# Fused linear attention and MLP: weight loads behind units 2, 3, 5 and 6, input loads in one fixed order

## Chip, cores and metric

One core of one Trainium2 chip. The metric is the device time of one execution in microseconds (us), as the median of the runs.

## What is computed

Two layers in a row on a batch of 8, with 8 heads, 576 positions and head width 64. The attention turns q and k into 256 positive features each and multiplies; the MLP normalises the joined heads (512 wide), goes up to 2048, cuts at zero, comes back to 512 and adds its input.

```python
def phi(x):
    proj = np.einsum('bhsd,df->bhsf', x, w_phi)
    proj = proj - np.max(np.abs(proj), axis=-1, keepdims=True)
    return np.concatenate([np.exp(proj), np.exp(-proj)], axis=-1)
q_p, k_p = (phi(q), phi(k))
kv = np.einsum('bhsf,bhsd->bhfd', k_p, v)
z = np.sum(k_p, axis=2)
num = np.einsum('bhsf,bhfd->bhsd', q_p, kv)
den = np.einsum('bhsf,bhf->bhs', q_p, z)[..., None] + 1e-06
x = num / den                      # then heads joined: (8, 576, 512)
xn = (x - mu) / np.sqrt(var + 1e-06) * g_ln
out = x + np.maximum(xn @ w_ch1, 0.0) @ w_ch2
```

## The kernel before

**Pairs, units, groups.** The batch is taken as four pairs of two. A pair's attention is 8 units (0 to 7 are pair 0, 8 to 15 pair 1, and so on); two units that share their loaded data are a group (g0 to g3 are pair 0, g4 to g7 pair 1). The 576 positions are 512 in the main loads and a rest of 64, the tails, which are loaded for many heads at once.

**One unit.** TensorE (PE) turns k and q with an identity (`qkT_ps`, L525; in pairs 1 to 3 a DMA transpose, L508, does it from a bf16 copy `qkb`). It projects them (`pm<-wbk` for k, `pm<-wbq` for q, L555, and `pt`, L648). VectorE (DVE) takes the maxima (L574), ScalarE (ACT) the exponentials (`EB`, `ea`), GpSimd (POOL) scales v into `vv` (L617 to L626), PE forms `kv` (L675) and then `num` (L704), DVE divides, and POOL writes the result into `x` (L728). The tails go the same way in small pieces: `xT_ps<-ident,kx` and `xT_ps<-ident,qx` (L394), then `px` (L404, L411).

**The MLP** of a pair takes 9 tiles of 128 rows in three rounds of three: centred tiles `xc`, turned to `xT`, the first layer `hT_ps` (L962, weights `w_98`), and the second layer `ch_ps` (L994, weights `w_99`). The MLP of one pair is interleaved with the attention of the next; the MLP of the last pair stands alone at the end.

**Buffers.** Inputs k and q lie in three buffers `qk_82`, `qk_83`, `qk_84`, v in `v_85`, `v_86`, `v_87`; group g uses buffer g modulo 3. The tails have two buffers each, by the pair's parity: `kx_90`, `qx_88`, `vx_92` for pairs 0 and 2, `kx_91`, `qx_89`, `vx_93` for pairs 1 and 3.

**Who loads.** Nearly all inputs are issued by SyncE (SP), whose queue is worked off in order: an issue that waits for a buffer holds all behind it, the DMA transposes and the stores too. The eight weight loads, 512 KB each as bf16, four of the first layer and four of the second, are issued by POOL (`load_w1`, `load_w2`, L284) from between its own work. A small memset of `kx_91` (L1139), put behind unit 4's `vv` on POOL, is the gate of pair 1's first loads.

**What sets the order.** `Order` (from L41) is a planner that runs while the kernel is built. Each step is added with an engine, an estimated time, a rank, and what it reads and writes; `run` then fixes the order of every engine by a list schedule over these estimates. A load is two steps: the issue on its queue, and the transfer on a resource "DMA" (SP and ACT loads) or "CAST" (POOL loads), whose times in the planner are independent of each other. While the flag `chained` is true, each SP load also writes a key "chain", so that loads are issued in the order in which the code adds them; after the loads of g5 it is set to False. The weights' places are a table from a unit to the loads that follow its `vv`:

```python
WEIGHTS = {0: (0,), 1: (1, 2), 2: (3,), 3: (4,), 4: (5,), 5: (6,), 6: (7,)}
```

Of the kernel before, what the change touches and what calls it, by code (L numbers as in the profile page):

```python
# [33 lines left out]
class Order:  # L34
# [73 lines left out]
    def run(self):  # L108
        waiting, free, room, events, done = {}, {}, self.room, [], []
        rows = False  # L110

        def offer(op):
            heapq.heappush(events, (op.ready, 1, op.number, op, None))

        for op in self.ops:
            for engine in op.alts:
                waiting.setdefault(engine, [])
                free.setdefault(engine, 0.0)
            if not op.left:
                offer(op)  # L120
        now = 0.0
        while events:
            now = events[0][0]
            while events and events[0][0] <= now + 1e-9:
                _, kind, _, op, _ = heapq.heappop(events)
                if kind == 1:
                    for engine in op.alts:
                        key = op.ready if engine in ("DMA", "CAST") else op.rank
                        heapq.heappush(waiting[engine], (key, op.number, op))
                elif kind == 0:  # L130
                    for name, n in op.release or ():
                        room[name] += n
            for engine, queue in waiting.items():
                if free[engine] > now + 1e-9 or not queue:
                    continue
                passed, held, op = [], set(), None
                while queue:
                    item = heapq.heappop(queue)
                    op = item[2]
                    if op.taken:  # L140
                        op = None
                        continue
                    if op.acquire is None or (
                        op.acquire[0] not in held and room[op.acquire[0]] >= op.acquire[1]
                    ):
                        break
                    held.add(op.acquire[0])
                    passed.append(item)
                    op = None
                for item in passed:  # L150
                    heapq.heappush(queue, item)
                if op is None:
                    continue
                op.taken, op.at = True, (now, engine)
                if op.acquire:
                    room[op.acquire[0]] -= op.acquire[1]
                end = now + op.alts[engine]
                if engine == "PE" and op.rows != rows:
                    rows = op.rows
                    end += 0.1  # L160
                lag = LAG[engine] if op.lag is None else op.lag
                free[engine] = end
                done.append((op, engine))
                heapq.heappush(events, (end, 2, op.number, op, None))
                heapq.heappush(events, (end + lag, 0, op.number, op, None))
                for o in op.users:
                    same = len(o.alts) == 1 and engine in o.alts
                    o.ready = max(o.ready, end + (0.1 if same else lag))
                    o.left -= 1
                    if not o.left:  # L170
                        offer(o)
        assert len(done) == len(self.ops)
        for op, engine in done:
            if op.emit:
                op.emit(engine)
        return now
# [3 lines left out]
def kernel(  # L180
# [71 lines left out]
    def early(kw):  # L252
        names = [name for name, _ in kw.get("release") or ()] + [kw.pop("frees", "")]
        return ahead[0] + (E_B if "B" in names else 0.0) + (E_A if "A" in names else 0.0)

    def add(engine, us, rank, emit, **kw):
        ahead_of = early(kw)
        sched.add(
            {engine: us}, rank, (lambda e: emit()) if emit else None, early=ahead_of, **kw
        )  # L260
# [16 lines left out]
    chained = [True]  # L277

    def dma(queue, rank, nbytes, dst, src, r=(), w=()):
        eng = ENG[queue]  # L280
        key = ("dma", len(sched.ops))

        def emit():
            eng.dma_start(out=dst() if callable(dst) else dst, in_=src() if callable(src) else src)  # L284

        chain = ["chain"] if queue == "SP" and chained[0] else []
        add(queue, {"SP": 0.55, "ACT": 0.55, "POOL": 0.84}[queue], rank, emit, r=r, w=(key, *w, *chain), lag=0.0)
        if queue == "POOL":
            add("CAST", 4.8, rank, None, r=(key,), w=w)
        else:  # L290
            rate = 240.0 if chained[0] else 330.0
            add("DMA", nbytes / rate / 1000.0, rank, None, r=(key,), w=w)

# [814 lines left out]
    load_tails(q, 0, [0, 1], "SP", 3.6)  # L1110
    moe_V = start(6)
    GATE = 4
    WEIGHTS = {0: (0,), 1: (1, 2), 2: (3,), 3: (4,), 4: (5,), 5: (6,), 6: (7,)}
    for n in range(NU + 2):
        V = start(n)
        step = start(n + 1) - V
        if n < NU:
            u = units[n]
            g, pair = u["g"], u["pair"]
            if n == 0:  # L1120
                a_trans(u, V)
            if u["uu"] == 0:
                if pair:
                    tails(g, V - 0.5 * step, None, True, g)
                    tails(g, V - 0.3 * step, [u["h"], u["h"] + 1], False, 64 + g)
                elif u["b"] == 0:
                    tails(g, V + 0.05, None, True, g)
                else:
                    tails(g, V, None, True, 8 + g)
            if pair == 0 and u["b"] == 1:  # L1130
                u["qjob"] = tails(g, V + 0.2 * step, [u["h"], u["h"] + 1], False, n)
            if pair:
                a_main(u, V, (1, 0))
            else:
                a_main(u, V, (1,))
            a_side(u, 1, V + 0.1 * step)
            if n == GATE:
                kx1 = kx_bufs[1]
                add("POOL", 0.1, V, lambda: nc.gpsimd.memset(kx1[:, :, 0:1], 0.0),  # L1139
                    r=[("vv", 0, n % 2)], w=[k_ for s_ in range(H) for k_ in tail_keys(1, s_, "k")])  # L1140
            for i_ in WEIGHTS.get(n, ()):
                after = [("vv", 0, n % 2)]
                if i_ < NW:
                    load_w1(i_, V, after)
                else:
                    load_w2(i_ - NW, V, after)
        if 0 < n <= NU:
            a_kv(units[n - 1], V + 0.2 * step)
        if n + 1 < NU:
            a_trans(units[n + 1], V + 0.3 * step)  # L1150
        if n < NU:
            if pair == 0:
                a_main(u, V + 0.35 * step, (0,))
            a_side(u, 0, V + 0.35 * step)
        if 0 < n <= NU:
            nums(units[n - 1], 0, V + 0.4 * step)
        if n < NU:
            a_feat(u, V + 0.5 * step)
        if 0 < n <= NU:
            w_ = units[n - 1]  # L1160
            nums(w_, 1, V + 0.6 * step)
            nums(w_, 2, V + 0.7 * step)
            if w_["pair"] == 0 and w_["b"] == 1:
                nums(w_, 3, V + 0.8 * step)
            pr, i = pairs[w_["pair"]], w_["i"]
            ahead[0] = E_X
            if w_["pair"] == 0 and i == 3:
                ahead[0] = E_X0
                for r in range(TILES0):
                    x_trans(pr, r, x_stats(pr, r, V), V)  # L1170
            if i == H - 1:
                pr["V"] = V + 0.9 * step
                ahead[0] = E_MOE
                moe_V = moe(pr, moe_V)
            ahead[0] = E_ATT
        gs = []
        if n % HG == 1 and n // HG + 3 != NGRP:
            gs.append(n // HG + 3)
        if n == GATE:
            gs = [NGRP] + gs  # L1180
        for g_ in gs:
            if g_ < NG:
                if g_ % NGRP == 0:
                    for i_, t_ in enumerate((k, q, v)):
                        load_tails(t_, g_ // NGRP, None, "SP", V + 0.1 * i_)
                for i_, t_ in enumerate((k, q, v)):
                    load_main(t_, g_, [0, 1], "SP", V + 0.5 + 0.1 * i_)
            if g_ == NGRP + 1:
                chained[0] = False
    ET = mybir.EngineType  # L1190
    with tc.manual_schedule(engines={ET.PE, ET.DVE, ET.Activation, ET.Pool, ET.SP}):
        sched.due()
# [31 lines left out]
```

## Time and profile before

| what | value |
|---|---|
| median of 3 runs | 400.43 us (400.22 to 401.17) |
| the profiled execution's own time | 402.7 us |
| its span, first to last instruction | 400.9 us |
| PE busy | 351.3 us (88%) |
| DVE, ACT, POOL busy | 278.4, 246.1, 210.8 us |
| moved by DMA | 52.69 MB, of it read from HBM 37.03 MB |
| mean granted TensorE clock | 0.982 |

The profiled execution is 2.3 us above the median. The shares are means over a run of unlike stages: start with only attention, a long middle in which attention and MLP alternate, and an end with only MLP. So the stretches are to be read one by one. A PE instruction shown as waiting for "issue" waits for something that the profile doesn't name.

### The profile page before, as it was taken

Reading aid. Unit: us, or ns where it says so; the run is one execution under the profiler, and the core shown is the slowest. Engines: PE = TensorE matmul, PEld = TensorE weight load, DVE = VectorE, ACT = ScalarE, POOL = GpSimd, SP = SyncE. Lnnn points to the kernel's source line nnn. Section 1 sums busy time; section 2 is a strip of 40 time slices with the busy share of each in tenths; the row PEclk is TensorE's granted clock in tenths of the full one; section 3 lists DMA queues with packets and bytes.
Section 4 is the critical chain, followed back from the end, with each engine's and each line's share of the span. In section 5 each row is a group of like instructions: output and inputs, shape, how many; then the busy total and the mean of one; then the engine's idle time right before and its main releaser. Section 6 shows DMA issues by size and latency. Waiting matters only on the chain. (4 is left out here: it accounts for less than half of the span.)

```text
span 400.9 us, 8845 instructions
## 1 busy us (share of the span) xinstructions
PE 351.3 (88%) x3283; PEld 208.7 (52%) x3332; DVE 278.4 (69%) x658; ACT 246.1 (61%) x511; POOL 210.8 (53%) x371
## 2 busy tenths in 40 slices
PE   3853586879999798999999999899999999999994
PEld 1632354536566454655655655465656545555541
DVE  3792989997779769887688898967768787010111
ACT  3993867769686743686777854966667505533310
POOL 4896796776544654975356675844445663000000
PEclk9996979999999999999999999999999999999999
DMA  7999799969547694692727524822200034110102
GB/s 196 318 228 250 164 220 316 274 158 225 158 91 117 171 226 124 151 191 54 213 54 210 132 41 105 173 42 54 52 28 28 29 92 93 39 54 26 51 31 78
DMA packets 88604, 52.69 MB, mean 131 GB/s; under 512 B 55024, under 2 KB 83824, under 8 KB 88560
## 3 DMA queue, kind: packets, MB, share of 16 engines
q1 hardware_dynamic: 83488, 47.07, 47.9%
q0 software_dynamic: 4224, 4.19, 6.3%
q10 hardware_dynamic: 848, 0.85, 0.7%
q8 instruction: 26, 0.43, 0.5%
q14 instruction: 18, 0.15, 0.1%
HBM read 37.03 MB, written 9.44 MB: 116 GB/s over the span
## 5 line engine op out<-in xcount | busy, mean ns | idle before, releaser
L962 PE MATMUL hT_ps<-xT,w 128*128 128x384 bf16 x768 | 150.2, 327 | 6.3 <-ACT KV L682 1.9
L994 PE MATMUL ch_ps<-w,hT 128*128 128x512 bf16 x536 | 141.2, 379 | 4.4 <-DVE numc L716 1.4
L972 ACT ACTIVATE hT<-hT_ps 128x384 bf16<-128x384 f32 x126 | 61.7, 492 | 74.4 <-PE hT_ps L962 73.8
L962 PEld LDWEIGHTS <-w 128*128 128x128 bf16 x768 | 71.4, 98 | 59.0 <-issue 8.7
L728 POOL TENSOR_TENSOR x<-numc,rden 128x192 bf16<-128x192 f32 (+1 forms) x112 | 51.0, 465 | 74.0 <-DVE rden L722 68.2
L574 DVE TENSOR_REDUCE m<-pm 128x8 f32<-128x1024 f32 x64 | 76.5, 1210 | 6.1 <-PE pm L555 5.9
L994 PEld LDWEIGHTS <-hT 128*128 128x128 bf16 x576 | 52.8, 98 | 50.7 <-DVE numc L716 2.5
L654 ACT ACTIVATE ea<-pt 128x1024 bf16<-128x1024 f32 x64 | 63.2, 1039 | 8.2 <-PE pt L648 6.8
L603 ACT ACTIVATE EB<-pm 128x1024 bf16<-128x1024 f32 x64 | 64.1, 1028 | 2.4 <-DVE m L574 2.4
L1001 DVE SCALAR_TENSOR_TENSOR o<-ch_ps,rstd,x 128x512 f32<-128x512 f32 x36 | 26.6, 742 | 52.7 <-PE ch_ps L994 39.7
L617 POOL TENSOR_TENSOR vv<-v,emk 128x512 bf16<-128x512 f32 x32 | 33.5, 1048 | 30.1 <-ACT emk L590 21.9
L710 DVE TENSOR_TENSOR numc<-num,emq 128x195 f32<-128x195 f32 (+1 forms) x96 | 32.9, 347 | 22.0 <-PE num L704 17.3
L970 DVE TENSOR_SCALAR hT<-hT_ps 128x384 bf16<-128x384 f32 x66 | 35.5, 542 | 8.2 <-PE hT_ps L962 7.2
L704 PEld LDWEIGHTS <-ea 128*128 128x128 bf16 x512 | 28.6, 99 | 18.7 <-issue 3.0
L704 PE MATMUL num<-KV,ea 128*128 128x65 bf16 x512 | 32.4, 196 | 3.1 <-DVE numc L716 1.9
L716 DVE TENSOR_TENSOR numc<-numc,num 128x195 f32<-128x195 f32 (+1 forms) x100 | 33.9, 344 | 1.5
L617 POOL TENSOR_TENSOR vv<-v,en 128x512 bf16<-128x512 f32 x32 | 33.4, 1045 | 0.4 <-DVE en L610 0.3
L861 POOL TENSOR_TENSOR xd<-x,mv 128x512 f32<-128x512 bf16 x19 | 20.8, 1094 | 11.1 <-DVE mv L848 10.0
L847 DVE BATCH_NORM_STATS2 st<-x 128x6 f32<-128x512 bf16 x36 | 24.3, 674 | 3.1 <-POOL x L728 3.1
L865 POOL TENSOR_TENSOR xc<-xd,gln 128x512 bf16<-128x512 f32 x19 | 25.3, 1331 | 1.5
L648 PE MATMUL pt<-qkT,wbk 128*128 128x512 bf16 x55 | 18.0, 397 | 8.0 <-DVE m L574 6.5
L675 PE MATMUL kv<-vv,EB 128*128 128x65 bf16 x512 | 24.8, 199 | 0.0
(67 smaller groups left out, 382.3 us busy)
## 6 DMA issues: line engine op xcount, KB each, us to landing
out_dram<-o SPq DMA_DIRECT2D x32, 256.0 KB, 2.4
qk<-in_k_dram SPq DMA_DIRECT2D x28, 256.0 KB, 4.1
v<-in_v_dram SPq DMA_DIRECT2D x28, 256.0 KB, 4.1
qk<-in_q_dram SPq DMA_DIRECT2D x26, 256.0 KB, 5.4
w<-in_moe_w_ch_dram POOLq DMA_DIRECT2D x8, 512.0 KB, 10.1
qk<-in_k_dram SPq DMA_DIRECT2D x2, 512.0 KB, 12.3
qk<-in_q_dram SPq DMA_DIRECT2D x2, 512.0 KB, 12.6
v<-in_v_dram SPq DMA_DIRECT2D x2, 512.0 KB, 15.0
```

The lines of the kernel that those rows point to most:

```text
L574: nc.vector.reduce_max(out=u["m", i].rearrange("p (c e) -> p e c", e=2), in_=u["pm", i], axis=AX.X, apply_absolute_value=True,)
L603: nc.scalar.activation(u["EB"][:, t].rearrange("p c f -> p (c f)"), u["pm", 1].rearrange("p e c f -> p (e c f)"), AF.Exp, scale=(1.0, -1.0 ...
L617: nc.gpsimd.tensor_tensor(out=u["vv"][:, t, 0:MX, 0:D], in0=vb[:, uu, :].rearrange("p (c d) -> p c d", d=D), in1=bcast(e[:, 0:MX], 2, D), ...
L654: nc.scalar.activation(u["EA"][:, t, :], u["pt"], AF.Exp, scale=(1.0, -1.0)[t])
L704: nc.tensor.matmul(ps[:, t, i, :], lhsT, rhs, start=(j == 0), stop=(j == len(terms) - 1))
L710: nc.vector.tensor_tensor(out=st["numc"][:, 0:nch], in0=st["ps"][:, 1], in1=bcast(em_of(), 2, D1), op=ALU.mult,)
L716: nc.vector.tensor_add(out=st["numc"][:, 0:nch], in0=st["numc"][:, 0:nch], in1=st["ps"][:, 0])
L728: nc.gpsimd.tensor_tensor(out=dst, in0=st["numc"][:, i : i + cnt, 0:D], in1=bcast(st["rden"][:, i : i + cnt], 2, D), op=ALU.mult,)
L962: nc.tensor.matmul(st["ps"][:, 0:cols], w1_sb[:, kc, jj * P : (jj + 1) * P], pr["xT", r][:, kc, 0:cols], start=(kc == 0), stop=(kc == KC - 1),
L970: nc.vector.tensor_relu(h_sb[:, 0:cols], st["ps"][:, 0:cols])
L972: nc.scalar.activation(h_sb[:, 0:cols], st["ps"][:, 0:cols], AF.Relu)
L994: nc.tensor.matmul(ch[t], hT[r, jj][:, rt * P : (rt + 1) * P], w2_sb[:, jj, :], start=(jj == 0), stop=(jj == JC - 1),)
```

## The change

It moves the weight loads in the table, two each behind units 2, 3, 5 and 6. It leaves `chained` true to the end, so all input loads are issued in the order of the code. And it changes the planner's estimates: one rate of 340 for SP and ACT loads where it was 240 or 330, 4.2 for a weight load where it was 4.8, and a transfer that starts while a weight load runs is taken to go at a quarter of its rate for that time. Since the planner's times change, all engines' orders change with them. The computation and every load's size stay.

```diff
@@ Order.run
                 op.taken, op.at = True, (now, engine)
                 if op.acquire:
                     room[op.acquire[0]] -= op.acquire[1]
-                end = now + op.alts[engine]
+                us = op.alts[engine]
+                if engine == "DMA" and free.get("CAST", 0.0) > now:
+                    shared = free["CAST"] - now
+                    us = 4.0 * us if 4.0 * us <= shared else us + shared * 0.75
+                end = now + us
@@ dma
         if queue == "POOL":
-            add("CAST", 4.8, rank, None, r=(key,), w=w)
+            add("CAST", 4.2, rank, None, r=(key,), w=w)
         else:
-            rate = 240.0 if chained[0] else 330.0
-            add("DMA", nbytes / rate / 1000.0, rank, None, r=(key,), w=w)
+            add("DMA", nbytes / 340.0 / 1000.0, rank, None, r=(key,), w=w)
@@
     GATE = 4
-    WEIGHTS = {0: (0,), 1: (1, 2), 2: (3,), 3: (4,), 4: (5,), 5: (6,), 6: (7,)}
+    WEIGHTS = {2: (0, 1), 3: (2, 3), 5: (4, 5), 6: (6, 7)}
@@
             if g_ == NGRP + 1:
-                chained[0] = False
+                pass
```

Lines of the changed kernel are 3 or 4 higher than those before. Three places show what it moves.

POOL, from unit 0's second `vv` (before) and from the end of unit 1 (changed) to the first weight loads that stand there. First before:

```order
L617 TENSOR_TENSOR vv<-v_85,en 128x8x64
L622 CAST vv<-en 128x8
L626 TENSOR_TENSOR vv<-vx_92,en 128x130
L284 DMA w_98<-in_moe_w_ch_dram 128x4x512
L617 TENSOR_TENSOR vv<-v_85,emk 128x8x64
L622 CAST vv<-emk 128x8
L626 TENSOR_TENSOR vv<-vx_92,emk 128x130
```

The change, where unit 2 (`v_86`) is the first with weights behind it:

```order
L731 TENSOR_TENSOR x_100<-numc,rden 128x64 x2
L620 TENSOR_TENSOR vv<-v_86,emk 128x8x64
L625 CAST vv<-emk 128x8
L629 TENSOR_TENSOR vv<-vx_92,emk 128x130
L620 TENSOR_TENSOR vv<-v_86,en 128x8x64
L625 CAST vv<-en 128x8
L629 TENSOR_TENSOR vv<-vx_92,en 128x130
L731 TENSOR_TENSOR x_100<-numc,rden 128x3x64
L288 DMA w_98<-in_moe_w_ch_dram 128x4x512 x2
```

The four loads of the first layer stood behind units 0, 1, 1 and 2 and stand behind 2, 2, 3 and 3; those of the second stood behind 3, 4, 5 and 6 and stand behind 5, 5, 6 and 6.

SP, from the last load of pair 0 (`v_85` of g3) on. Before:

```order
L284 DMA v_85<-in_v_dram 128x4x256
L284 DMA kx_90<-in_k_dram 64x8x64 x2
L284 DMA kx_91<-in_k_dram 64x8x64
L284 DMA qk_82<-in_k_dram 128x2x256
L284 DMA kx_91<-in_k_dram 64x8x64
L284 DMA qk_82<-in_k_dram 128x2x256
L284 DMA qx_89<-in_q_dram 64x8x64
L284 DMA qk_82<-in_q_dram 128x2x256
```

The change:

```order
L288 DMA v_85<-in_v_dram 128x4x256
L288 DMA kx_91<-in_k_dram 64x8x64 x2
L288 DMA qx_89<-in_q_dram 64x8x64 x2
L288 DMA vx_93<-in_v_dram 64x8x64 x2
L288 DMA qk_83<-in_k_dram 128x2x256 x2
L288 DMA qk_83<-in_q_dram 128x2x256 x2
L288 DMA v_86<-in_v_dram 128x2x256 x2
L288 DMA qk_84<-in_k_dram 128x2x256 x2
```

Tails of pair 2 (`kx_90`, and `qx_88` further on) and k and q of g6 (`qk_82`) stood ahead of pair 1's first group (`qk_83`); now pair 1's tails and then g4 and g5 come first.

PE, around the turning of pair 0's q tails (`qx_88`). Before, between unit 2's last `num` and unit 3's `kv`, behind unit 4's `pm<-wbk`:

```order
L704 MATMUL num<-KV,ea_94 128x65
L394 LDWEIGHTS qx_88
L394 MATMUL xT_ps<-ident,qx_88 128x128
L670 LDWEIGHTS EBx
L670 MATMUL kv<-vv,EBx 128x130
```

The change, between unit 3's `pm<-wbk` and `pm<-wbq`:

```order
L558 MATMUL pm<-wbk,qkT 128x128
L407 LDWEIGHTS xT_488
L407 MATMUL px<-wbk,xT_488 128x256
L397 LDWEIGHTS qx_88
L397 MATMUL xT_ps<-ident,qx_88 128x128
L558 LDWEIGHTS qkT
L558 MATMUL pm<-wbq,qkT 128x128
```

The step now comes about a unit earlier. In the same way unit 2's turning of k (`qk_83`) stands ahead of unit 1's `pm<-wbk`, where it came behind its `pm<-wbq`.

## Rows read from the trace of the kernel before

**Rows 1.** Chain of work that ended last: its shares by line.

```profile
by line: PE ch_ps L994 7.5%; PE hT_ps L962 6.6%; issue 0.2%; DVEq L1219 0.2%; DVE o L1001 0.2%
```

**Rows 2.** Busy time by stretch: stretch, length, PE, PEld, DVE, ACT, POOL, clock, DMA share, GB/s.

```profile
28.00:32.00 4.00, 0.51 (x5) 0.26 (x4) 2.57 (x10) 3.86 (x8) 3.98 (x10) 0.97 1.19 232
32.00:36.00 4.00, 0.54 (x8) 0.57 (x9) 0.24 (x2) 0.00 (x0) 4.00 (x9) 0.50 1.17 248
36.00:40.00 4.00, 3.11 (x46) 2.28 (x45) 1.76 (x3) 2.15 (x6) 0.22 (x2) 0.68 1.17 255
40.00:44.00 4.00, 2.31 (x46) 1.78 (x43) 3.99 (x15) 3.26 (x7) 1.37 (x4) 1.00 0.86 165
44.00:48.00 4.00, 2.42 (x40) 1.71 (x39) 3.90 (x9) 4.00 (x9) 3.70 (x6) 1.00 0.57 122
48.00:52.00 4.00, 2.12 (x24) 1.70 (x24) 4.00 (x10) 2.49 (x8) 3.92 (x5) 0.60 0.99 238
52.00:56.00 4.00, 3.79 (x42) 2.71 (x41) 2.94 (x11) 3.34 (x8) 3.98 (x10) 0.54 1.25 207
57.00:100.00 43.00, 34.59 (x392) 21.74 (x394) 38.34 (x94) 31.87 (x69) 31.06 (x55) 1.00 1.02 244
100.00:395.00 295.00, 283.46 (x2468) 163.07 (x2505) 199.36 (x455) 174.16 (x362) 136.70 (x230) 1.00 0.40 97
```

**Rows 3.** Timeline of PE: start, length, instruction, in brackets the wait before it.

```profile
12.78 0.61 PE L555 MATMUL pm<-wbk,qkT 64*128 64x128 bf16 x8 [0.52 <-DVE qkT L275]
...
24.99 0.40 PE L555 MATMUL pm<-wbq,qkT 64*128 64x128 bf16 x8 [0.98 <-ACT ea L654]
...
35.46 0.37 PE L394 MATMUL xT_ps<-ident,qx 128*128 128x128 bf16 x2 [6.75 <-issue]
...
39.33 0.40 PE L525 MATMUL qkT_ps<-ident,qk 128*128 128x128 bf16 x4 [0.89 <-DMA qk<-in_k_dram]
...
42.89 0.40 PE L525 MATMUL qkT_ps<-ident,qk 128*128 128x128 bf16 x4 [1.56 <-DMA qk<-in_q_dram]
...
57.24 0.40 PE L555 MATMUL pm<-wbk,qkT 64*128 64x128 bf16 x8
```

**Rows 4.** Loads of q tails and of g3's k: issues, then time to landing.

```profile
L284 SPq DMA_DIRECT2D qx<-in_q_dram x2: 762/1602/2441, 18.4 to 19.2; - x2
...
DMA to landing us min/median/max: 14.5/15.3/16.1
...
L284 SPq DMA_DIRECT2D qk<-in_k_dram x1: 3834/3834/3834, 21.8 to 21.8; - x1
...
DMA to landing us min/median/max: 17.5/17.5/17.5
```

**Rows 5.** Loads of g1, its first k and last v: issue, then time to landing.

```profile
L284 SPq DMA_DIRECT2D qk<-in_k_dram x1: 367/367/367, 7.8 to 7.8; - x1
...
DMA to landing us min/median/max: 5.1/5.1/5.1
...
L284 SPq DMA_DIRECT2D v<-in_v_dram x1: 584/584/584, 10.2 to 10.2; - x1
...
DMA to landing us min/median/max: 6.3/6.3/6.3
```

**Rows 6.** Timeline of POOL: the first weight loads.

```profile
13.74 0.94 POOL L284 DMA_DIRECT2D w<-in_moe_w_ch_dram  x1
...
19.30 1.55 POOL L284 DMA_DIRECT2D w<-in_moe_w_ch_dram  x2
```

**Rows 7.** Timeline of SP: last load of pair 0, first of the next, first transpose.

```profile
26.64 5.15 SPq L284 DMA_DIRECT2D v<-in_v_dram  x1
43.38 1.97 SPq L284 DMA_DIRECT2D kx<-in_k_dram  x3
...
64.88 4.46 SPq L508 DMA_TRANSPOSE qkT<-qkb  x1
```

**Rows 8.** DMA queue of the weight loads: packets, MB, share of 16 engines.

```profile
q0 software_dynamic: 4224, 4.19, 6.3%
```

## The prediction

> **What bounds the kernel now.** I read the chain that ended last first, then the busy time by stretch, then PE's timeline where the stretches show holes. The chain is PE alone [rows 1], the MLP of the last pair. From 100 to 395 us PE is busy 283.46 of 295 us, 96% [rows 2]. No other engine comes near, so work that reaches PE earlier in the first 100 us moves the end by as much, as long as the late order keeps PE fed. From 57 to 100 us PE is busy 34.59 of 43, and DVE, busy 38.34, is the fuller one. The hole lies before: from 28 to 36 us PE does 1.05 us of work, and DVE falls to 0.24 us in the second half of that.
>
> PE's timeline says what the hole is [rows 3]. Its queue stands 6.75 us at the turning of pair 0's q tails, then 0.89 us for k of g3 and 1.56 us for q of g3: 9.2 us in three waits. The first is named "issue", but the loads show the cause: the second q-tail load went out at 19.2 and landed 16.1 us later, at 35.3, and the turning starts at 35.46. k of g3, issued at 21.8, took 17.5 us to 39.3; its turning starts at 39.33 [rows 3, 4]. All this time the DMA share stands at 1.17 to 1.19 [rows 2]: the transfers are late because the engines are full. Three weight loads were issued at 13.74, 19.30 and just behind [rows 6], and three more (by the table) behind units 2, 3 and 4.
>
> What input loads do without them is seen just before: k, q, v, k, q, v of g1, 256 KB each, land from 7.8 + 5.1 = 12.9 to 10.2 + 6.3 = 16.5 us [rows 5], five steps in 3.6 us, 0.72 us per 256 KB.
>
> **Part by part.**
>
> *Weights behind units 2, 3, 5, 6: the three waits.* No weight is issued before unit 2's vv, about 24.5 us: unit 3's `pm<-wbq` stands at 24.99 [rows 3]. Between 16.5 and the end of the q tails lie 2 MB of inputs (three loads of 512 KB in g2, 512 KB of tails in small pieces). They took 18.8 us with weights beside them. At g1's pace they take 8 x 0.72 = 5.8 us and the q tails land at 22.3, the lower end; if nothing were gained they land at 35.3, the upper end. The near row is g1's, for the same kind of load with nothing beside it; I add one more 0.72 for each 256 KB of tails (smaller pieces) and about a us for SP's issues, and take 25. PE now reaches that step before unit 3's `pm<-wbq`, which waited to 24.99 for ACT anyway: about 0.5 us of the 6.75 stays. k and q of g3 follow, 512 KB each. At g1's pace they land at 26.5 and 28. But the moved weights begin about here, and beside weights k took 39.3 - 35.3 = 4.0 us; so q lands between 28 and 33. PE wants both before unit 4's `pm<-wbq`, at about 28.5. I take 1.5 us of wait (0 to 4.5). Removed: 9.2 - 0.5 - 1.5 = **7.2 us** (4 to 9).
>
> Here a rule speaks against counting on more. The rows show that beside weights 512 KB took 4.0 us where two steps of 0.72 were enough [rows 4, 5]. The Trainium skill, "DMA: Bandwidth & Descriptors", section "Queues, rings and completion order", says that each DMA engine goes round-robin between the queues that have work, a packet at a time. By that rule a weight load slows whatever input load it meets, early or late, and the change only chooses which; the trace agrees that it slows them (2.8 times). The sum above by that rule alone would have q of g3 at 33, and 4 us saved in place of 7.2.
>
> *The planner's new rate: PE's order at the start.* Inputs are now taken to come sooner, so unit 2's k is turned before unit 1's `pm<-wbk`. That stood at 12.78 [rows 3]; k of g1 lands at 12.9 [rows 5], and four matmuls of about 0.6 us stand between, so it moves to about 13.5. Unit 3's turnings move ahead of unit 0's `kv` in the same way. Cost **+0.7 us** (0 to 1.5).
>
> *The clock.* After the long wait the granted clock is 0.50 and 0.68, and again 0.60 and 0.54 from 48 to 56 [rows 2], so partly the lower of the two levels, 1.2 GHz. Most of that lies beside a full DVE. From 52 to 56 PE itself is full, 3.79 of 4 us at 0.54; at 2.4 GHz that work needs 3.79 x 0.54 = 2.05. Without the 6.75 us hole ahead and with units following closely I expect most of this back: **-1.5 us** (0 to -3).
>
> *One fixed order on SP.* SP ends pair 0's loads at 26.64 + 5.15 = 31.8 and starts the next at 43.38 [rows 7], because tails of pair 2, which need a buffer of pair 0, come next in its queue. Ahead of g4 it then sends those, and k and q of g6. Now pair 1's tails and g4 come first and wait only for the gate behind unit 4. That would bring pair 1 forward. But all six early weight loads now fall into the same stretch. I take **0** beyond the shift of pair 0 (-4 to +4): the earlier start of these loads covers the weights. If it does not, unit 8 starts late and the shift is partly lost (second rival).
>
> *POOL's issues.* Eight, as before; 0.94 and 1.55 us of them [rows 6] leave POOL's first units and come back behind later ones: 0, hidden as long as POOL's vv isn't the last thing that `kv` waits for, at most 1 us either way. The late orders differ little in kind, and PE's last round is row for row the same: 0, with 2 us either way for the 11.5 us that PE idles from 100 to 395.
>
> Sum: -7.2 + 0.7 - 1.5 = **-8.0 us**. Against the profiled execution's own time that is 402.7 to 394.7; it lay 2.3 us above the median, so for the median 400.43 - 8.0 = **392.4 us**.
>
> **The rivals.**
>
> *More than the waits (387).* DVE is full from 40 to 52 [rows 2]; if pair 1's data come 8 us earlier as well, the 8.4 us that PE idles from 57 to 100 shrink by about half, 4 us, and q of g3 meets no weight (1.5 more): -13. For it: SP's 11.6 us of standing still. Against it: DVE stays the fuller engine there. Chance 0.15, 385 to 389.
>
> *The gain is given back at the start of pair 1 (396.6).* The bytes are the same, and the DMA engines were nearly full. Below about 1.18 they fell only in three stretches: 0.86, 0.57, 0.99 from 40 to 52 [rows 2], which is (0.32 + 0.61 + 0.19) x 4 / 1.18 = 3.8 us of room. A weight load takes 6.3% of 400.9 / 8 = 3.2 us of all engines [rows 8], six of them 19 us, and these now meet pair 1's loads and the first transpose, issued at 64.88 [rows 7]. If DMA bounds until then, unit 8 comes 3.8 us earlier and not 8, and PE runs out of MLP work: -3.8. The Trainium skill says in the same page, "Issuing engines are not separate DMA queues", that loads issued by different engines end on the same 16 DMA engines; moving them between POOL's places adds no room, and by that rule alone this is the case. For it: the shares above 1.1 on both sides. Against it: about 1 MB of pair 2's and g6's loads no longer goes first. Chance 0.22, 395 to 399.
>
> *Nothing (400.4).* The waits move to the new places on PE and cost the same. For it: PE now wants tails and g3 a unit sooner. Against it: five weight loads less ahead of them, 16 us of the engines. Chance 0.06.
>
> *Slower: PE stands before unit 8 for second-layer weights (405).* Their last two loads now both follow unit 6's vv. Sixteen `ch_ps` matmuls now stand in PE's queue ahead of unit 8's `pm<-wbk`, where none did. Unit 7's `pm<-wbk` stood at 57.24 [rows 3]; 7 us earlier and some 12 us of PE work on, PE wants these weights at about 62. Issued at about 50, they land in time if they take 12 us, and 5.5 late at the 17.5 us of a crowded load [rows 4]. PE's queue is in order, so all of pair 1 waits behind. From 20 us to landing on, the 8 us are lost; at 25 us it is +5. Against it: no load in the trace took 20. Chance 0.09.
>
> **How the numbers follow.** A difference of 0.3%, 1.2 us, is about what a measurement of this kernel can tell from no change. The forecast, 389 to 395, has 0.48; with the two faster rivals faster has 0.85, same 0.06, slower 0.09. The forecast's own range takes its terms' ends without adding them all up. The range of 385 to 399 takes in both faster rivals and leaves out 0.15 and their outer edges.
>
> **What would show it.** Right: the wait of 6.75 us gone, no PE wait over 2 us from 24 to 40, unit 7's `pm<-wbk` near 50, a clock near 1.00 from 32 to 56, DMA share without the dip at 44 to 48. Waits for qk loads of 3 to 4 us near 30 would say that the moved weights still meet g3. PE idle between 55 and 75 us, waiting on `qkT`, would mean the second rival; a wait at the first `ch_ps` the last. If PE idles clearly more than 11.5 us after the first 95 us or so, the new late order is at fault, and my 0 for it was wrong.

## The result and the profile after

The changed kernel takes 389.86 us (median of 4 runs, 386.62 to 391.34); the kernel before, on the same chip, 400.8 us (400.22 to 401.26). The ratio is 0.9717 with a 95% interval of 0.9648 to 0.9786: 10.9 us faster. The forecast was 392.4 us, within 385 to 399. A second set of runs gave 389.98 us and 0.9707 (0.964 to 0.9774).

The profiled executions lie further apart than the medians: 402.7 us before is above its median, 386.62 us after is the fastest of four. The profile before also lacks 49 of 3332 matmul records and the one after none, so PE's idle time late in the two is not compared; starts of instructions are.

The busy time by stretch of the changed kernel, with the columns of [rows 2]:

```profile
28.00:32.00 4.00, 3.11 (x52) 2.16 (x52) 3.13 (x11) 4.00 (x13) 4.00 (x10) 1.00 1.22 215
32.00:36.00 4.00, 2.13 (x40) 1.52 (x36) 4.00 (x11) 4.00 (x10) 3.99 (x9) 1.00 1.18 179
36.00:40.00 4.00, 3.12 (x36) 1.91 (x37) 3.97 (x14) 4.00 (x9) 4.00 (x11) 0.84 1.13 197
40.00:44.00 4.00, 3.28 (x60) 2.78 (x58) 3.93 (x10) 3.00 (x8) 3.62 (x6) 0.73 0.77 169
44.00:48.00 4.00, 2.99 (x38) 2.27 (x38) 4.00 (x15) 3.42 (x6) 2.35 (x5) 1.00 1.08 184
57.00:100.00 43.00, 41.37 (x441) 25.43 (x439) 39.37 (x103) 34.17 (x71) 31.41 (x57) 1.00 0.97 213
```

From 28 to 36 us PE does 5.24 us of work where it did 1.05, and DVE, which had stood, is full from 32 to 48. The DMA share is no lower than before from 28 to 36, 1.22 and 1.18: the engines are as busy, with other transfers. From 57 to 100 us PE idles 1.63 us where it idled 8.41 [rows 2].

PE's timeline at the steps of [rows 3], and the first matmul of the second layer:

```profile
25.55 0.27 PE L397 MATMUL xT_ps<-ident,qx 128*128 128x128 bf16 x2 [0.89 <-DMA qx<-in_q_dram]
...
30.56 0.61 PE L528 MATMUL qkT_ps<-ident,qk 128*128 128x128 bf16 x8
...
49.12 0.40 PE L558 MATMUL pm<-wbk,qkT 64*128 64x128 bf16 x8
...
65.59 1.46 PE L997 MATMUL ch_ps<-w,hT 128*128 128x512 bf16 x6 [0.21 <-ACT hT L975]
```

The kernel before, at unit 8's `pm<-wbk` and the first matmuls of the second layer, then the changed kernel at unit 8:

```profile
74.29 0.40 PE L555 MATMUL pm<-wbk,qkT 64*128 64x128 bf16 x8
...
80.99 0.82 PE L994 MATMUL ch_ps<-w,hT 128*128 128x512 bf16 x3 [0.39 <-DVE numc L716]
```

```profile
72.52 0.40 PE L558 MATMUL pm<-wbk,qkT 64*128 64x128 bf16 x8
```

The second layer now comes first: it starts 15.4 us earlier, unit 8 only 1.8. The wait of 6.75 us is 0.89; g3 is turned in one go at 30.56 without a wait; unit 7's `pm<-wbk` stands at 49.12 instead of 57.24, 8.1 us earlier. The loads behind it, the second q tails, k and q of g3 (issue, then time to landing, as in [rows 4]):

```profile
L288 SPq DMA_DIRECT2D qx<-in_q_dram x1: 1152/1152/1152, 18.6 to 18.6; - x1
...
DMA to landing us min/median/max: 6.8/6.8/6.8
...
L288 SPq DMA_DIRECT2D qk<-in_k_dram x1: 507/507/507, 20.2 to 20.2; - x1
...
DMA to landing us min/median/max: 6.5/6.5/6.5
...
L288 SPq DMA_DIRECT2D qk<-in_q_dram x1: 2023/2023/2023, 20.8 to 20.8; - x1
...
DMA to landing us min/median/max: 7.4/7.4/7.4
```

They land at 25.4, 26.7 and 28.2 us: 6.5 to 7.4 us after their issue, where q tails and k of g3 took up to 16.1 and 17.5. The timelines of POOL and SP, first weights, first load of pair 1, first transposes:

```profile
25.56 1.68 POOL L288 DMA_DIRECT2D w<-in_moe_w_ch_dram  x2
...
37.76 1.29 SPq L288 DMA_DIRECT2D kx<-in_k_dram  x2
...
59.38 9.79 SPq L511 DMA_TRANSPOSE qkT<-qkb  x2
```

The weights begin when these inputs have all but landed: from 27 to 28 us their queue moves 0.01 MB of the 0.34 MB that move in all. SP starts pair 1 at 37.76 instead of 43.38 and reaches the first transpose at 59.38 instead of 64.88 [rows 7].

So the early rows looked much as forecast, but for the clock from 36 to 44 us. The experiments ask whether the cause was the one I gave: that weights moved out of the way end the waits, and that the rest of the change is worth about nothing.

### The profile page after: what moved, and what is told of

Read it like the earlier page. It is cut to its first block, busy times and chain, and to the rows that moved or that the text cites. A ratio compares the mean times of both kernels' runs of the same rounds, so it can differ in the third digit from the quotient of the medians.

```text
span 384.8 us, 8899 instructions
## 1 busy us (share of the span) xinstructions
PE 351.2 (91%) x3332; PEld 205.6 (53%) x3332; DVE 275.1 (71%) x657; ACT 248.1 (64%) x516; POOL 204.0 (53%) x365
## 5 line engine op out<-in xcount | busy, mean ns | idle before, releaser
L997 PE MATMUL ch_ps<-w,hT 128*128 128x512 bf16 x576 | 148.1, 379 | 0.7 <-DVE hT L973 0.5
L975 ACT ACTIVATE hT<-hT_ps 128x384 bf16<-128x384 f32 x129 | 63.1, 491 | 68.0 <-PE hT_ps L965 67.4
L731 POOL TENSOR_TENSOR x<-numc,rden 128x192 bf16<-128x192 f32 (+1 forms) x112 | 52.1, 476 | 60.8 <-DVE rden L725 58.0
L1004 DVE SCALAR_TENSOR_TENSOR o<-ch_ps,rstd,x 128x512 f32<-128x512 f32 x36 | 26.5, 743 | 54.1 <-PE ch_ps L997 41.3
L973 DVE TENSOR_SCALAR hT<-hT_ps 128x384 bf16<-128x384 f32 x63 | 34.0, 545 | 8.5 <-PE hT_ps L965 7.8
L707 PEld LDWEIGHTS <-ea 128*128 128x128 bf16 x512 | 27.5, 98 | 19.7 <-issue 4.2
L707 PE MATMUL num<-KV,ea 128*128 128x65 bf16 x512 | 31.5, 195 | 4.7 <-ACT KV L685 2.0
L864 POOL TENSOR_TENSOR xd<-x,mv 128x512 f32<-128x512 bf16 x17 | 18.7, 1097 | 11.2 <-DVE mv L851 10.8
L651 PE MATMUL pt<-qkT,wbk 128*128 128x512 bf16 x64 | 19.7, 390 | 4.7 <-DVE m L577 2.1
L678 PE MATMUL kv<-vv,EB 128*128 128x65 bf16 x512 | 23.9, 196 | 0.0
L868 POOL TENSOR_TENSOR xc<-xd,gln 128x512 bf16<-128x512 f32 x17 | 22.6, 1328 | 1.3
```

The costliest lines, as they stand in the source:

```text
L707: nc.tensor.matmul(ps[:, t, i, :], lhsT, rhs, start=(j == 0), stop=(j == len(terms) - 1))
L731: nc.gpsimd.tensor_tensor(out=dst, in0=st["numc"][:, i : i + cnt, 0:D], in1=bcast(st["rden"][:, i : i + cnt], 2, D), op=ALU.mult,)
L973: nc.vector.tensor_relu(h_sb[:, 0:cols], st["ps"][:, 0:cols])
L975: nc.scalar.activation(h_sb[:, 0:cols], st["ps"][:, 0:cols], AF.Relu)
L997: nc.tensor.matmul(ch[t], hT[r, jj][:, rt * P : (rt + 1) * P], w2_sb[:, jj, :], start=(jj == 0), stop=(jj == JC - 1),)
```

## The experiments

The ratio in each is to the kernel before on the same chip, whose median was 402 to 403 us there. "Table" is the weights' places, "chain" the one fixed order of loads, "estimates" the planner's numbers.

**Undoing or doing parts with the orders kept.** In the next four, every engine keeps the order of the kernel named; only weight issues are put behind another unit's `vv` on POOL, or some loads are put further back on SP.

*x1*, the kernel before with the weights moved:

```diff
+    held, AFTER = {}, {2: (0, 1), 3: (2, 3), 5: (4, 5), 6: (6, 7)}
+        if hold is not None:
+            held[hold], emit = emit, lambda: None
...
+            if t == 0:
+                for i_ in AFTER.get(n, ()):
+                    held[i_]()
```

> The kernel before, with every engine's order kept and only the eight weight issues moved on POOL, to behind units 2, 2, 3, 3, 5, 5, 6, 6. Theory A (the waits come from weight bytes ahead of pair 0's inputs): the waits for q tails and for k and q of g3 fall from 9.2 us to under 3, the q tails land near 25, and the time falls by 5 to 8 us, to 393 to 396. Theory B (the gain is in the new orders): the waits may go, but the time falls by under 2 us, since the old order has nothing to fill the time with.

Measured 403.73 us, ratio 1.0034 (0.999 to 1.0078): no gain. The three early waits are gone and unit 5's `pm<-wbk` stands at 33.61 instead of 39.84. But the whole machine stands later on. Waits from 56 to 67 us (us in total, times, longest), and busy time by stretch:

```profile
DVE qkb L275 <- DMA qk<-in_q_dram: 8.5, 1, 8.5
...
PE num L712 <- ACT KV L690: 7.8, 1, 7.8
```

```profile
60.00:64.00 4.00, 0.00 (x0) 0.00 (x0) 0.00 (x0) 0.00 (x0) 0.00 (x0) 0.66 1.17 246
64.00:68.00 4.00, 1.98 (x16) 1.30 (x16) 3.09 (x8) 1.58 (x6) 1.00 (x3) 0.50 1.13 313
68.00:72.00 4.00, 4.00 (x42) 2.90 (x40) 2.76 (x11) 1.60 (x6) 1.55 (x4) 0.56 1.23 216
```

No engine does anything from 60 to 64 us. At the head of DVE's queue stands the cast of g4's q, which is still in flight; behind it wait the maxima that ACT needs, and so PE. SP had sent pair 2's tails and g6 ahead of g4. Then PE runs at 0.50 and 0.56, that is mostly at 1.2 GHz, until 72 us. What pair 0 gained, pair 1's start gave back.

*x2*, the changed kernel with the weights issued at their old places:

```diff
+    held, AFTER = {}, {0: (0,), 1: (1, 2), 2: (3,), 3: (4,), 4: (5,), 5: (6,), 6: (7,)}
```

> The changed kernel, with every engine's order kept and only the eight weight issues moved back, to behind units 0, 1, 1, 2, 3, 4, 5, 6. Theory A: the q tails land late again, near 35, PE waits 8 to 10 us for them ahead of unit 3's q projection, and the time goes back to 396 to 400. Theory B: it stays within 3 us of the changed kernel, under 393.

Measured 399.27 us, ratio 0.9944 (0.9906 to 0.9982), 9.3 us above the changed kernel run beside it. The first of PE's waits from 16 to 57 us:

```profile
PE xT_ps L402 <- DMA qx<-in_q_dram: 6.3, 1, 6.3
```

With the changed kernel's orders, early weights bring the old wait back. Busy time from 57 to 100 us, x1's row first, then x2's, says what they leave alone:

```profile
57.00:100.00 43.00, 31.25 (x307) 19.59 (x307) 30.38 (x76) 25.46 (x58) 26.16 (x46) 0.84 1.02 225
```

```profile
57.00:100.00 43.00, 40.30 (x428) 24.82 (x427) 38.73 (x98) 33.79 (x73) 31.74 (x60) 0.98 0.77 199
```

PE is busy there for 34.59 us in the kernel before and 41.37 in the changed one. With the changed kernel's orders it is about as full with the weights at their old places (40.30); with the old orders it is not with the weights at the new ones (31.25; x3 and x4 below have 35.62 and 32.38). So in these orders the weights' places carry the gain before 57 us (x2's unit 7 starts at 59.99, later than before the change), and the orders carry the one behind it. *x3*, the kernel before with g6's k and q sent after g5, and pair 2's tails after g7:

```diff
+                after="g5" if g == 6 and t is not v else None,
+                after="g7" if pair == 2 and t is not v else None,
```

> The kernel before, with only SP's queue altered: k and q of g6 go behind g5, and pair 2's k and q tails behind g7; all other orders and the weights stay. If SP's order is a part of the gain (theory C), pair 1's loads start at about 37 in place of 43, PE's idle time from 57 to 100 us shrinks, and the time falls by 2 to 5 us. If the DMA engines or DVE bound that stretch anyway (theory A), it falls by under 1.5 us.

Measured 400.42 us, ratio 0.9966 (0.9931 to 1.0001): some 1.4 us, not clear of no change. *x4* joins x1 and x3:

> The kernel before with all orders kept, but for the weight issues (as in x1_weights_moved) and SP's queue (as in x3_loads_deferred) together. Theory A2: x1 gained its waits but gave them back where DVE stood 8.5 us for q of g4 ahead of unit 8's copy, because SP still sent pair 2's tails and g6 first. Then the two together are worth more than the sum of each alone (+1 and -2 us): that wait falls under 3 us and the time to 393 to 397. Theory B (only new orders of PE, DVE and ACT bring the gain): 398 to 402.

Measured 398.37 us, ratio 0.987 (0.9805 to 0.9934). By these ratios x1 gave +1.4 and x3 -1.4, and together they give -5.2 us: the load order does end x1's stall. But the time missed the 393 to 397 of theory A2 and lies in theory B's range, 6 to 7 us above the changed kernel by the ratios and 8 by the medians. Waits from 57 to 80 us:

```profile
ACT qkb L273 <- DMA qkT<-qkb: 7.0, 1, 7.0
POOL qkb L275 <- DMA qkT<-qkb: 5.3, 1, 5.3
```

Casts for the next group now stand at the heads of the queues of ACT and POOL until a transpose frees their buffer. I read that as again an order made for other arrivals; no run shows it.

**The three parts with all orders laid out anew.** The rest of the runs use the kernels as the planner makes them. The changed kernel once more, as a base:

> The changed kernel once more. Its four times lay between 386.6 and 391.3, the lower ones with a mean clock nearer to 1. If the spread is the clock's (theory A), time and mean clock go together again, some 0.5 us for each 1 us at the lower level, and a profile with a mean clock near 0.98 shows stretches at 1.2 GHz that the first one lacks. Otherwise the times differ at the same clock.

389.98 us. Its profile against the first one of the same kernel, 24 to 57 us, this run's row first:

```profile
24.00:57.00 33.00, 25.72 (x328) 18.36 (x324) 29.83 (x84) 29.63 (x66) 29.45 (x60) 0.79 1.07 229
```

```profile
24.00:57.00 33.00, 24.52 (x349) 17.02 (x347) 31.25 (x90) 31.18 (x67) 30.86 (x63) 0.95 1.09 234
```

The same orders, at a mean granted clock of 0.79 or 0.95 in this stretch: PE is busy longer for fewer matmuls, and the execution takes 389.07 instead of 386.62 us. At 0.5 us for each us at the lower level, 33 x (0.95 - 0.79) = 5.3 us were to be expected; it is 2.45. Unit 7's `pm<-wbk` in this run, at the same clock of 0.79 from 24 to 57 us that the profile before has:

```profile
50.83 0.40 PE L558 MATMUL pm<-wbk,qkT 64*128 64x128 bf16 x8
```

*Table alone*, which is x1's move with orders laid out for it:

```diff
-    WEIGHTS = {0: (0,), 1: (1, 2), 2: (3,), 3: (4,), 4: (5,), 5: (6,), 6: (7,)}
+    WEIGHTS = {2: (0, 1), 3: (2, 3), 5: (4, 5), 6: (6, 7)}
```

> The kernel before with the new weight table alone; the planner lays out all orders anew, with its old estimates, and SP's loads are free of the chain after g5. Theory A2: SP sends loads out of turn again, an engine stands for g4's data near 55 to 65, 397 to 403. If the table with any new plan is enough: 389 to 393.

Measured 400.41 us, ratio 0.9954 (0.9918 to 0.9991), as theory A2 had it: from 55 to 82 us POOL waits 5.3 us for a load of v, and PE 4.0 us for a transpose. *Table and chain*, with the old estimates:

```diff
+    WEIGHTS = {2: (0, 1), 3: (2, 3), 5: (4, 5), 6: (6, 7)}
...
-                chained[0] = False
+                pass
```

> Table and chain, with the planner's old estimates (240 for a load, 4.8 for a weight load, no slowing of one by the other). Theory A2: the gain is in weights and load order, so 389 to 395. If the new estimates carry a part of it, by an order that fits the real landings: 395 to 399.

Measured 394.79 us, ratio 0.9787 (0.9741 to 0.9834), at the upper end of the first theory's range. *Table and estimates*, the changed kernel with the chain ended after g5:

```diff
-                pass
+                chained[0] = False
```

> The changed kernel with the chain ended after g5 again; table and estimates stay. Theory A2: loads go out of turn, an engine stands for g4 for 4 to 8 us, 394 to 400. If the chain doesn't matter beside new estimates: 388 to 392.

Measured 395.64 us, ratio 0.9801 (0.975 to 0.9853). The time is in theory A2's range, but its reason is not there: from 55 to 75 us no engine waits longer than 1.8 us. DVE's timeline, result tiles 2 and 3 of the first pair's MLP:

```profile
98.16 0.75 DVE L1004 SCALAR_TENSOR_TENSOR o<-ch_ps,rstd,x 128x512 f32<-128x512 f32 x1
...
117.60 0.72 DVE L1004 SCALAR_TENSOR_TENSOR o<-ch_ps,rstd,x 128x512 f32<-128x512 f32 x1
```

The changed kernel has them at 97.83 and 112.84, so most of the loss falls between the two; what causes it stays open. Up to here I believed that the three parts only work together. The next three runs were to complete the table, and they ended that.

*Chain alone*:

```diff
-                chained[0] = False
+                pass
```

> Only the one fixed order of SP's loads, with the old weight table and the old estimates; all orders laid out anew. If the three parts need each other, this gives little, as the queue-only version did (-1.5 to -2): 0 to -3 us against the kernel before, and the wait of some 6 us at the turning of the q tails stays, since the early weights still stand in their way. If the load order is what gives back or keeps the gain by itself, 5 us or more faster.

Measured 395.7 us, ratio 0.9854 (0.9803 to 0.9904): twice the most that I expected, and over the 5 us named for a load order that gains by itself. The early wait stays, as expected, among PE's waits from 16 to 57 us:

```profile
PE xT_ps L394 <- issue: 5.2, 1, 5.2
```

Most of the gain comes later. DVE's timeline, result tiles 2 and 5 of the first pair's MLP, of the kernel before and of this one:

```profile
112.42 0.75 DVE L1001 SCALAR_TENSOR_TENSOR o<-ch_ps,rstd,x 128x512 f32<-128x512 f32 x1 [0.27 <-PE ch_ps L994]
...
152.95 0.74 DVE L1001 SCALAR_TENSOR_TENSOR o<-ch_ps,rstd,x 128x512 f32<-128x512 f32 x1
```

```profile
112.48 0.74 DVE L1001 SCALAR_TENSOR_TENSOR o<-ch_ps,rstd,x 128x512 f32<-128x512 f32 x1
...
146.73 0.72 DVE L1001 SCALAR_TENSOR_TENSOR o<-ch_ps,rstd,x 128x512 f32<-128x512 f32 x1
```

Tile 2 is level, tile 5 is 6.2 us ahead. What it is in the new order between 112 and 147 us that saves this, I did not isolate.

*Estimates alone*, old table, chain ended after g5:

```diff
-                end = now + op.alts[engine]
+                us = op.alts[engine]
+                if engine == "DMA" and free.get("CAST", 0.0) > now:
+                    shared = free["CAST"] - now
+                    us = 4.0 * us if 4.0 * us <= shared else us + shared * 0.75
+                end = now + us
...
-            rate = 240.0 if chained[0] else 330.0
-            add("DMA", nbytes / rate / 1000.0, rank, None, r=(key,), w=w)
+            add("DMA", nbytes / 340.0 / 1000.0, rank, None, r=(key,), w=w)
```

> Only the planner's new estimates, with the old weight table and the chain ended after g5. If the estimates help only where the loads then come as estimated, -1 to +3 us against the kernel before: PE's orders count on inputs that still come late, a wait of 5 us or more for q tails or g3 stays before 40 us. If the better filling with MLP work is a gain of its own (the first second-layer matmul near 66 us instead of near 79), 3 us or more faster.

Measured 394.4 us, ratio 0.9823 (0.9766 to 0.9879). The weights' table is the old one, and 7.1 us are gone. PE's timeline at the q tails, then the load of the second of them:

```profile
33.28 0.61 PE L558 MATMUL pm<-wbk,qkT 64*128 64x128 bf16 x8 [0.60 <-DVE m L577]
33.82 0.84 PE L707 MATMUL num<-KV,ea 128*128 128x65 bf16 x12
35.29 0.37 PE L397 MATMUL xT_ps<-ident,qx 128*128 128x128 bf16 x2 [0.63 <-DMA qx<-in_q_dram]
```

```profile
L288 SPq DMA_DIRECT2D qx<-in_q_dram x1: 4122/4122/4122, 19.0 to 19.0; - x1
...
DMA to landing us min/median/max: 16.2/16.2/16.2
```

The tails land at 19.0 + 16.2 = 35.2 us, as late as in the kernel before (35.3), and the wait is 0.63 us instead of 6.75. The planner now takes a load beside weights to be slow, and puts other work ahead of the turning: unit 5's `pm<-wbk`, at 33.28 here, stood behind it before, at 39.84. The early hole was one of order as well as of loads.

But the estimates alone are not the orders of PE alone. SP's timeline, the first loads of pair 1:

```profile
40.12 2.72 SPq L288 DMA_DIRECT2D kx<-in_k_dram  x4
42.89 3.59 SPq L288 DMA_DIRECT2D qx<-in_q_dram  x2
46.53 1.88 SPq L288 DMA_DIRECT2D vx<-in_v_dram  x2
48.45 3.84 SPq L288 DMA_DIRECT2D qk<-in_k_dram  x2
```

In the order that the planner builds here, pair 1's tails and g4's k (`qk_83`) stand ahead of g6 (`qk_82`), with only pair 2's k tails still in front, much as the chain would have it; with the table alone it is the same. With table and estimates, g6 and pair 2's tails stay ahead of g4 as in the kernel before. So "chain" off does not mean one load order, and of the 7.1 us I can't say how much is SP's order and how much PE's.

*Chain and estimates with the old table*, the same weights' places and chain as in x2:

```diff
-    WEIGHTS = {2: (0, 1), 3: (2, 3), 5: (4, 5), 6: (6, 7)}
+    WEIGHTS = {0: (0,), 1: (1, 2), 2: (3,), 3: (4,), 4: (5,), 5: (6,), 6: (7,)}
```

> The changed kernel but for the weight table, which is the old one; all orders laid out anew for it (the run with the changed kernel's orders and the old places gave -2.3 us). If the weights' places carry the early gain, 398 to 401 us, 1 to 4 us faster than the kernel before and 8 or more slower than the changed one. If the orders can make up for the old places, under 395.

Measured 392.95 us, ratio 0.9787 (0.9738 to 0.9836). PE's timeline shows the tails turned without any wait, at 34.47; their load:

```profile
34.47 0.40 PE L397 MATMUL xT_ps<-ident,qx 128*128 128x128 bf16 x2
```

```profile
L288 SPq DMA_DIRECT2D qx<-in_q_dram x1: 3392/3392/3392, 20.2 to 20.2; - x1
...
DMA to landing us min/median/max: 12.7/12.7/12.7
```

Against x2, 399.27 us, the places of the weights are the same and the order laid out for them is worth 6.3 us. All together (the kernel before has 17.75 us in the last column):

| table | chain | estimates | us | ratio to before | PE busy, 57 to 80 us |
|---|---|---|---|---|---|
| new | | | 400.41 | 0.9954 | 17.12 |
| | new | | 395.7 | 0.9854 | 17.59 |
| | | new | 394.4 | 0.9823 | 19.98 |
| new | new | | 394.79 | 0.9787 | 17.26 |
| new | | new | 395.64 | 0.9801 | 20.98 |
| | new | new | 392.95 | 0.9787 | 20.94 |
| new | new | new | 389.86 and 389.98 | 0.9717 and 0.9707 | 22.04 and 20.89 |

Of 402 us the parts alone give 1.8, 5.9 and 7.1 us, 14.8 in all; together they give 11.4 to 11.8. What is lost lies between chain and estimates, which give 5.9 and 7.1 us alone and 8.6 together; since the estimates alone already reorder SP's loads, the two may in part be the same remedy, but no run separates that. The intervals of the single runs, some 2 us either way, leave the size of the loss loose. The table's share on top of the other two is 392.95 - 389.9 = 3.0 us, outside the spread of either kernel's runs (392.49 to 393.18, against 386.62 to 391.65).

The last column shows a second place where the estimates act. All four kernels with new estimates have 20 to 22 us of PE work from 57 to 80, the three without 17.1 to 17.6. The row with table and chain, beside that of the changed kernel:

```profile
57.00:80.00 23.00, 17.26 (x167) 10.58 (x166) 18.04 (x55) 13.69 (x30) 13.23 (x27) 0.93 1.17 239
```

```profile
57.00:80.00 23.00, 22.04 (x226) 13.82 (x225) 21.29 (x56) 16.42 (x41) 18.81 (x31) 1.00 1.11 254
```

In the first, unit 8's `pm<-wbk` starts earlier (69.47 against 72.52) and the second layer later (78.97 against 65.59). With the new estimates the planner puts the MLP of pair 0 where PE would wait for pair 1. That is not the whole of the gain: chain alone and table with chain stand at 17.59 and 17.26, no more than the kernel before, and are 5.9 and 8.6 us faster.

**Is it pair 1's inputs that bound what is left?** The changed kernel with the gate one unit earlier:

```diff
-    GATE = 4
+    GATE = 3
```

> The changed kernel with the gate of pair 1's first loads behind unit 3 instead of unit 4, so that they start some 5 us earlier. DVE is busy 31.25 of the 33 us from 24 to 57 in the changed kernel; if it, and not the inputs of pair 1, bounds that stretch, no gain: 388 to 392, as the changed kernel. If pair 1's inputs still bound the start of pair 1, 2 to 4 us faster. If the earlier loads meet the first weights and g3 again, 2 us or more slower, with a wait for k or q of g3 of 2 us or more near 30 us.

Measured 391.57 us (390.8 to 393.2), ratio 0.9767 (0.9706 to 0.9829): as the changed kernel, if anything 1.6 us slower. SP's timeline, and busy time by stretch:

```profile
33.69 1.33 SPq L288 DMA_DIRECT2D kx<-in_k_dram  x2
...
59.51 6.92 SPq L511 DMA_TRANSPOSE qkT<-qkb  x2
```

```profile
40.00:57.00 17.00, 12.79 (x151) 9.09 (x153) 15.88 (x48) 13.47 (x29) 14.07 (x27) 0.80 1.16 250
```

Pair 1's loads start 4.1 us earlier, and the first transpose goes out at 59.51 instead of 59.38. DVE is busy 15.88 of 17 us. Starting these loads earlier brings nothing before 57 us; DVE's full queue is the near candidate for what bounds that stretch, which I did not test by making DVE faster. No version tried beats the changed kernel.

## Why the prediction was right, and where its reasons were not

The number was right to 2.5 us and the early part came out almost as summed. That the total agrees is in part luck: the account of which part of the change does it was wrong, and what the orders gain after 57 us was put at nothing.

- **The three waits, -7.2.** They went further than I took: 9.2 us became 0.89. q tails, k and q of g3 landed at 25.4, 26.7 and 28.2, for 25, 26.5 and 28 to 33 in the working. q of g3 met almost no weight: POOL issued the first two only at 25.56, and their queue had moved 0.01 MB by 28 us, when q was all but in. The Trainium skill, "DMA: Bandwidth & Descriptors", section "Queues, rings and completion order", has each DMA engine go round-robin between queues with work; by that rule alone I had q of g3 at 33. The trace doesn't speak against the rule: next to nothing of the weights was under way yet.
- **But not by the weights' places alone.** I ascribed all of this term to the table. Alone the table is worth 1.8 us, on top of the rest 3.0. The estimates alone, and chain with estimates, end the wait with the weights at their old places, by order; x1 ends it by places and gains nothing. In the changed kernel itself the places are needed, as x2 shows, since its orders count on them.
- **PE's order at the start, +0.7.** As a cost this was there: units 1, 3 and 4 have their `pm<-wbk` 1.1, 1.2 and 2.0 us later, the last above the 1.5 of its range. Unit 5's, in front of which the waits lay, is 6.5 us earlier. The step that failed is that I looked for the new estimates' effect in this one place and on the cost side only: alone, with the load order that comes with them, they gain 7.1 us, and the second layer now fills PE ahead of unit 8.
- **One fixed order on SP, 0 (-4 to +4).** Wrong: -5.9 us alone, with the orders it brings; on top of the other two (0.9801 - 0.9717) x 402 = 3.4 us by the ratios, 5.7 by the medians. With the old orders it prevents x1's stall of all engines for g4's q. In table and estimates without it no such stall is seen, and most of the loss comes between 98 and 118 us; why stays open.
- **Late orders, 0 (±2).** Wrong with the chain alone, where 6.2 us come between tiles 2 and 5. In the changed kernel result tile 0 is 17.5 us earlier (72.72 against 90.25), the last 16.2 (378.86 against 395.03), in the second profile 14.8 and 13.7: there the gain was made by about 90 us. The 11.5 us that PE was said to idle from 100 to 395 us were too many: 37 of the missing matmul records lie there (2468 matmuls to 2505 weight loads), and x1 and x3, with the same late order and all their records, idle 8.6 and 8.0.
- **The clock, -1.5.** In the first profile of the changed kernel only 36 to 44 us, at 0.84 and 0.73, is below 1.00 between 28 and 56; the second has 0.79 for 24 to 57. The two executions differ by 2.45 us, so the term has about this size, but it is no steady gain, and the reason I gave doesn't hold: the hole is gone in both, and in the second the clock from 24 to 57 us is 0.79, as in the kernel before.
- **The sum, -8.0** was met at unit 7's `pm<-wbk`, 8.1 us earlier. In the second profile, at the clock of the kernel before, it is 6.4 us earlier: that is -7.2 + 0.7 = -6.5, and the 1.7 between the two executions go with the clock. More came after it, from 57 to 100, where PE's idle time fell by 6.8 us (5.8 in the second profile). These spans are 16.1 and 13.6 us shorter than the one before, more than the 10.9 us of the medians, as the profile before is a slower execution and the first one after the fastest. The other step that failed is the zero for the one order on SP and for the late orders. The first rival (387 us) had the place and about the size, and the result lies between it and the forecast, but its mechanism was another: pair 1 was to come 8 us earlier, and unit 8 comes 1.8 us earlier, in the second profile 0.9 later (75.21). What fills PE is the second layer of pair 0, 15.4 us earlier, and x2 shows that this comes with the orders and not with the weights' places. I had seen these sixteen `ch_ps` ahead of unit 8, but only as a danger.
- **Gain given back (396.6)** did not happen to the change, and is just what happened to x1. I had priced it as lack of room on the DMA engines. The Trainium skill's section "Issuing engines are not separate DMA queues" of the same page says that DMAs end on the same 16 DMA engines whichever engine started them. From this I had it that moving loads adds no room; that agrees with the DMA share, 1.22 and 1.18 from 28 to 36, where it was 1.19 and 1.17. But 10.9 us came with as full DMA engines: which transfer goes first, what PE does meanwhile, and who waits at a queue's head, decided.
- **PE stands before unit 8 for second-layer weights (405)** was not seen: the first `ch_ps` waits 0.21 us, for ACT.

## What to carry to other kernels

Where a planner fixes all orders, one edit of its numbers is an edit of every queue: price its estimates as a change of their own, and test each part both with the old orders kept and with orders laid out anew, since the two answers differ by 3 to 6 us here. Then read the orders that each version got: a part that is switched off by name can come back through the plan, as the load order did with the estimates alone. A wait for a late load can be ended by an earlier load or by other work put ahead of it, so its length doesn't say what an earlier load is worth. Where a gain early in the run vanishes, look at the head of each in-order queue further on (in x1 some 25 us), for an instruction placed there for data that used to have time to come.

## What the runs showed of the hardware

The granted clock of one stretch is no property of the kernel. From 24 to 57 us it was 0.95 in one execution of the changed kernel and 0.79 in another with the same orders, and the four runs of the first set, 386.62, 388.7, 391.34 and 391.02 us, had mean clocks of 0.994, 0.986, 0.977 and 0.982. I had not expected a spread of 1.2% in time beside such clocks, as the kernel before, 400.22 to 401.26 us there, spread by 0.3% in that set. In the later sets it spread too, from 398.54 to 406.24 us at mean clocks of 0.954 to 0.984, so the narrow spread was one of few runs.
